# Linear attention with a gated unit: first-pass transfers queued behind weight loads, output-weight sums in steps, q feature steps spaced wider

## The chip, the cores and the metric

The kernel runs on one core of a Trainium2 chip. The metric is the device time of one execution in microseconds. TensorE (PE) multiplies into PSUM banks; VectorE (DVE), ScalarE (ACT) and GpSimd (POOL) do the element work; SyncE (SP) issues every transfer from one queue. Each engine works its queue off in the order in which the program was built.

## The reference

Both branches read the same layer-normed rows `xn` (2048 rows of 1024). The result is `x + s * silu(B)`.

```python
def _A_ref(x, wqkv, w_phi, wo):                  # x is xn
    q, k, v = ...(x @ wqkv)                      # 32 heads of 32
    pq = einsum("bhsd,hdf->bhsf", q, w_phi); pk = einsum(..., k, w_phi)
    phi_q = concatenate([softmax(pq), softmax(-pq)], -1)
    phi_k = concatenate([softmax(pk), softmax(-pk)], -1)
    kv = einsum("bhsf,bhsd->bhfd", phi_k, v); z = phi_k summed over s
    o = (phi_q @ kv) / (phi_q @ z + 1e-6)
    return o.reshape(B, S, D) @ wo
def _B_ref(x, w_gate, w_up, w_down):             # 1024 -> 3584 -> 1024
    return (sigmoid(x @ w_gate) * (x @ w_up)) @ w_down
```

## The kernel before, in words

**Products.** All large products are made by a two-by-two block scheme with seven products in place of eight. The products are called B11, B21, T2, T3, T4, T1 and B22, in this order; their operands are blocks or sums of blocks. fp32 operands are split in a high and a low part (`split`, L133 on ACT for the high part, L134 on DVE for the low one), and each product is three matmuls (`mm3`, L142 to L144), high by high, high by low, low by high. A group of twelve matmuls, four k steps of three, makes the share of one product in one PSUM bank; four groups, into banks 0 to 3 (named bank0_101 to bank3_104), make one operation. B11, T2, T3 and T1 start their banks anew; the others add to them. So before a bank is written again, its content must have been fetched by ACT or DVE.

**Stages.** The list `ops` sets TensorE's order: projection 0 (V, K and Q with seven operations each, for the first half of the rows), the first pass over the 14 tiles of the gated unit (two operations each, B11 and B21), projection 1 (the second half of the rows), the second and the third pass; then the down product and the attention output. The change touches the second half of projection 0 and the first pass.

**Ticks and steps.** After each group `tick` advances a clock and takes the entries of `plan` due then; `later(n, f)` makes such an entry n ticks ahead. What an entry issues is tied, by `tc.issue_after(last_mm[0])`, to TensorE's queue alone. `tc.issue_after(i)` orders only those instructions of its block that stand in the queue of i's engine. Otherwise a scheduler, with a model of the times, sets the order on each engine, so an entry's transfers and its element work can be put far ahead of their tick. `queue2` ties a step's transfers behind `last_load`, the last load or store so marked.

**Background steps around the change.**

- Q folds (`fold`, L350 on): the q weights times w_phi, summed on POOL (L291 to L294) and stored to `wf_d` (L345), in the first operations after the opening.
- Output weights (`o_sums`, L319 on): for k = 0 to 3, four blocks of `wo` are loaded into the halves of slots 52 and 53 (L322), split and stored as they are for three products, then summed on POOL and split and stored for the other four (L328). All of it is issued in one entry.
- Next rows (`x_stats` and `x_moments`): row loads (L178) and statistics (L694, L695) for the eight row tiles of the second half; then `x_pair`, four times, 12 ticks apart: loads (`x_in`, L724 and L727), scaling on DVE (`x_apply`, L733, four a pair), sums on POOL (L270, L234), stores.
- q features (`q_steps`, L808 on): 16 chains, 6.5 ticks apart: load, extremes (L546, L547), spread (L556, L557), exponentials on ACT (L560), sums and reciprocals (L565, L566), stores to `e_d` and `r_d`.

**Fetches.** In projection 0, `proj_out` fetches the banks: B11 and B21 on ACT (L520, L523), the others on DVE (`evac`, L517). In the first pass B11's banks are copied by ACT and stored (`keep_bank`, L1235, L1236), B21's banks 0 and 1 go through a sigmoid on ACT and banks 2 and 3 through a multiplication on DVE (`h_direct`, L1268, L1270). `glu_load` (L393) loads the pass's weights, up to four operations ahead.

Of the kernel before, what the change touches and what calls it, by code (L numbers as in the profile page):

```python
# [3 lines left out]

# [45 lines left out]
def hedgehog_glu_kernel(  # L50
# [66 lines left out]
    def whole(i):  # L117
        return slots[i].rearrange("p a n -> p (a n)")
# [36 lines left out]
    def tick():  # L155

        clock[0] += 1
        with tc.issue_after(last_mm[0]):
            glu_group()
        for f, a in sorted(plan.pop(clock[0], []), key=lambda fa: fa[0] is fetch_operand):  # L160
            with tc.issue_after(last_mm[0]):
                f(*a)

    side = deque()

# [121 lines left out]
    def w_sums(keep, a11, a12, a21, a22):  # L287

        for i, b in ((B11, a11), (B21, a12), (T4, a22)):
            keep(i, b)  # L290
        nc.gpsimd.tensor_add(a22, a21, a22)  # L291
        nc.gpsimd.tensor_sub(a21, a11, a21)
        nc.gpsimd.tensor_sub(a11, a22, a11)
        nc.gpsimd.tensor_sub(a12, a12, a11)  # L294
        for i, b in ((T2, a11), (T3, a21), (T1, a22), (B22, a12)):
            keep(i, b)
# [19 lines left out]

    o_split = Ring((54, 36, 37, 38))

    def o_sums(k, bs):  # L319

        for b, (f, h) in zip(bs, ((0, 0), (0, 1), (1, 0), (1, 1))):
            nc.sync.dma_start(b, wo[(k + 4 * h) * P:(k + 4 * h + 1) * P, f * HB:(f + 1) * HB])  # L322

        def keep(i, b):
            r = o_split.next()
            o = slots[r].bitcast(F32R)
            split((o[:, 0], o[:, 1]), b)
            nc.sync.dma_start(wo_d[i, k], whole(r))  # L328

        w_sums(keep, *bs)  # L330

    FB = ((0, 0), (0, 1), (1, 0), (1, 1))

# [49 lines left out]
    def glu_load(n):  # L383

        if n == len(ops) or ops[n][0] != "glu" or n in wraw:
            return True
        _, p, f, i = ops[n]
        if p == 1 and f in FLY:
            return True
        src = wg_d[summed.index(i), f] if i in summed else w_gu[f + NJ * (i == T4), int(i != B11)]  # L390
        if p == 0:
            r = gr.next()
            nc.sync.dma_start(whole(r), src)  # L393
            wraw[n] = halves(r)
            return True
        if (p, f, i) == (1, 0, T2):
            raw_free.extend(halves(41, 42, 39, 40))
        if len(raw_free) < 2:
            return False
        wraw[n] = [raw_free.popleft() for _ in range(2)]  # L400
        for s, o in enumerate(wraw[n]):
            last_load[:] = [nc.sync.dma_start(o, src[:, s * HB:(s + 1) * HB]).ins]
        if (p, f, i) == (1, 1, T4):
            spare.extend(halves(43, 44))
            raw_free.extend(spare)
        return True
# [152 lines left out]
    def exponentials(e):  # L559
        nc.scalar.activation(e, e, AF.Exp)  # L560
# [247 lines left out]
    def q_steps(at, t, hb):  # L808

        def load():  # L810
            p, e = hold[:] = qf_raw.next(), whole(qf_e.next())
            nc.sync.dma_start(p, qkv_d[Q, t, hb])

        def first():
            hold.append(extremes(f"q{t}{hb}", hold[0]))

        def rest():
            r = inverses(hold[2], hold[1])
            nc.sync.dma_start(r_d[t, hb], r)
            nc.sync.dma_start(e_d[t, hb], hold[1])  # L820

        hold = []
        for n, f in ((0, load), (4, first), (5, lambda: spread(hold[2], *hold[:2])), (7, lambda: exponentials(hold[1])),
                     (9, rest)):
            later(at + n, f)

    def q_task(t, hb):
# [459 lines left out]
    def begin_projection(c):  # L1287

        if c == 0:
            for k in range(4):  # L1290
                queue2(4 * (4 + 2 * k), o_sums, k, halves(52, 53))
            return
        for t in range(EARLY):
            k_steps(1 + 72 * t // EARLY, 0, t)
        for n in range(5):
            queue2(17 + 8 * n, glu_sums, *sums.popleft(), halves(43, 44))
# [30 lines left out]
    for n, (kind, c, what, i) in enumerate(ops):  # L1327
        if n < 8:
            continue
        ws = ready[n]  # L1330
        if kind == "proj":
            if n == 8 or (c and (what, i) == (PROJ[0], B11)):
                begin_projection(c)
            first_slot = (XO1 if c else XO)[i]
            xo = run(first_slot, 4)
            for u in range(4):
                if i in opening:
                    pbank[u] = pmm.next()
                us = slice(u * P, (u + 1) * P)
                for k in range(4):  # L1340
                    mm3(pbank[u], (xo[:, k, 0, us], xo[:, k, 1, us]), pair(ws[k]),
                        i in opening and k == 0, k == 3, skip_group_check=True)
                step()
                proj_out(c, what, i, u, pbank[u])
                if c and (what, i) == (Q, B22):
                    seed(0, u)
                if u < 3:
                    tick()
            flow["used"] += 4
            while prep():  # L1350
                pass
            if what == Q:
                if c == 0:
                    if i == T2:
                        load_outer(B11, 1)
                if c:
                    m = order.index(i)
                    if m < 6:
                        load_outer((T2, T2, T3, T3, T4, T4)[m], m % 2)
                    if i == T1:  # L1360
                        phase = 1
                        fetch(0)
                    if i == B22:
                        block("x1", 4, 4, F32)
                        m1 = halves(4, 5, 6, 7)
            tick()
            continue

        phase, f = c, what
        m = f * len(PASSES[phase]) + PASSES[phase].index(i)  # L1370
        if m == 0:
            if phase == 0:
                step(1000)
                for b in (0, 2, 6):
                    block(f"x{b}", 4 * b, 4, F32)
            begin_pass(phase)
        if (phase, i) in ((1, T2), (2, T1)):
            fetch(f + 1)
        for b in range(4):
            s, th = divmod(b, 2)  # L1380
            w = [h.rearrange("p (k m) -> p k m", m=P) for h in pair(ws[s])]
            xo = run(XG[i][th], 4)
            for k in range(4):
                mm3(banks[b], (w[0][:, k], w[1][:, k]), (xo[:, k, 0], xo[:, k, 1]),
                    i in (B11, T1) and k == 0, k == 3, skip_group_check=True)
            if i in (B11, T2, T3):
                keep_bank((B11, T2, T3).index(i), f, b)
            elif i == B21:
                h_direct(0, f, b)
            elif i == T4:  # L1390
                h_direct(0, f + NJ, b)
                seed(f + 1, b)
            elif i == T1:
                h_added(1, f + NJ, fetched[f][2], b)
            else:
                h_added(1, f, fetched[f][1], b)
            if th:
                flow["used"] += 1
                while prep():
                    pass  # L1400
            if b < 3:
                tick()
        if flow["item"] == len(items) and flow["made"] - flow["used"] < NW:
            hfree.extend(ws)
            while wfree and down_prep():
                pass

        if phase == 0:
            for o in {20: (B11,), 21: (B21,), 22: (T2,), 26: (T3, T4), 27: (T1, B22)}.get(m, ()):
                load_operand(XO1[o], xo_d[o])  # L1410
            if m == 27:
                block("p", 36, 2, F32R)
                block("p2", 38, 1, F32R)
        elif phase == 1 and (f, i) == (NJ - 2, T4):
            load_outer(T1, 0, lead=2)
        elif phase == 1 and f == NJ - 1:
            if i == T2:
                load_outer(T1, 1, lead=2)
                load_outer(B22, 0, lead=2)
            elif i == T3:  # L1420
                load_outer(B22, 1, lead=2)
            else:
                for b in (3, 5):
                    block(f"x{b}", 4 * b, 4, F32)
                uvfree.extend(halves(12, 13, 14, 15, 20, 21, 22, 23, 47, 51, 45, 46))
                hs_r.items = halves(48, 49, 50)
                phase = 2
                fetched.clear()
                fetch(0)
        elif phase == 2 and f == NJ - 2 and i == T1:  # L1430
            wfree.extend(range(16, 20))
        tick()
# [266 lines left out]
```

## Time and profile before

| | us |
|---|---|
| median of 3 runs | 2381.9 (2381.58 to 2384.36) |
| the profiled execution | 2384.26 |
| its span | 2382.5 |
| PE busy | 2364.6 (99%) |
| DVE busy | 1630.9 (68%) |
| ACT busy | 1046.5 (44%) |
| POOL busy | 957.6 (40%) |

A row of the timeline has the start, the duration, the engine, the line, the operation with its tiles, and in square brackets how long the engine was idle before it and who ended that. "<-issue" stands where the profile shows no waited-for event. SPq rows are transfers as SP issues them. A row of the waits has the engine and line, what it waited for, and us in total, times, and the longest. A row of the windows has the stretch, its length, then busy us (and instructions) of PE, PE's weight loads, DVE, ACT and POOL, the granted TensorE clock as a share of full speed, the DMA share and GB/s. A row of the groups has busy us and the mean ns of one. A row of the transfers has the count, KB each, and the median us from issue to landing.

### The profile page before, as it was taken

The page shows a single profiled execution, that of the slowest core. Times are in us where ns is not written, and L with a number is a line of the kernel's source. Part 1 is how long each engine was busy: PE and PEld are TensorE (multiplying, and loading weights), DVE is VectorE, ACT ScalarE, POOL GpSimd, SP SyncE. Part 2 cuts the span into 40 slices and gives each one's busy share as a digit, 9 for nine tenths or more (in the row PEclk, how much of TensorE's full clock was granted, in tenths as well). Part 3 has the DMA queues.
Part 4 walks back from the last instruction along what each step waited for, and adds up shares of the span by engine and source line. Part 5 has one row for each costly group of instructions (what it writes and reads, how often), then busy time and mean ns, then how long its engine had stood idle before and what let it go on. Part 6 is the DMA issues. An engine that isn't in the chain of part 4 may idle for free. (4 is left out here: it accounts for less than half of the span.)

```text
span 2382.5 us, 32056 instructions
## 1 busy us (share of the span) xinstructions
PE 2364.6 (99%) x10972; PEld 1970.0 (83%) x10972; DVE 1630.9 (68%) x2103; ACT 1046.5 (44%) x1595; POOL 957.6 (40%) x617
## 2 busy tenths in 40 slices
PE   9999999999999999999999999999999999999999
PEld 8887887888888888888888888888888888888887
DVE  8635847875577946577766633344888998877776
ACT  7333334364433545455555422223444334355553
POOL 0223227721032034444411587863333334423566
PEclk9999999999999999999999999999999999999999
DMA  8799989985587787677765999977666766876665
GB/s 294 251 319 339 372 332 346 340 302 188 176 287 259 256 292 243 212 255 249 234 203 189 345 382 379 346 266 252 213 220 227 234 221 209 283 264 235 200 208 180
DMA packets 287732, 631.45 MB, mean 265 GB/s; under 512 B 36688, under 2 KB 36944, under 8 KB 282960
## 3 DMA queue, kind: packets, MB, share of 16 engines
q1 hardware_dynamic: 287568, 629.40, 76.5%
q8 instruction: 86, 1.41, 0.2%
q14 instruction: 78, 0.64, 0.1%
HBM read 376.31 MB, written 252.97 MB: 264 GB/s over the span
## 5 line engine op out<-in xcount | busy, mean ns | idle before, releaser
L142 PE MATMUL bank<-x,w 128*128 128x512 f32 x2352 | 917.2, 390 | 4.6 <-ACT fc L1235 3.3
L143 PE MATMUL bank<-x,w 128*128 128x512 f32 x2352 | 916.6, 390 | 0.0
L144 PE MATMUL bank<-x,w 128*128 128x512 f32 x2352 | 914.9, 390 | 0.0
L134 DVE TENSOR_TENSOR w<-fa,w 128x512 fp32r<-128x512 f32 (+1 forms) x437 | 415.6, 957 | 206.4 <-ACT w L133 190.4
L133 ACT CAST w<-fa 128x512 fp32r<-128x512 f32 (+1 forms) x437 | 297.6, 685 | 543.0 <-PE bank L143 353.2
L142 PEld LDWEIGHTS bank<-x,w 128*128 128x128 f32 x2352 | 442.3, 188 | 97.3 <-ACT fc L1235 4.2
L144 PEld LDWEIGHTS bank<-x,w 128*128 128x128 f32 x2352 | 442.3, 188 | 92.3 <-DVE w L134 0.4
L143 PEld LDWEIGHTS bank<-x,w 128*128 128x128 f32 x2352 | 442.4, 188 | 90.6
L142 PE MATMUL bank<-w,x 128*128 128x512 f32 x708 | 278.8, 394 | 2.8 <-DVE fc L517 2.1
L143 PE MATMUL bank<-w,x 128*128 128x512 f32 x708 | 276.8, 391 | 0.9 <-DVE w L1092 0.9
L144 PE MATMUL bank<-w,x 128*128 128x512 f32 x708 | 276.6, 391 | 0.0
L142 PEld LDWEIGHTS bank<-w,x 128*128 128x128 f32 x708 | 133.4, 188 | 30.4 <-ACT p L133 2.5
L144 PEld LDWEIGHTS bank<-w,x 128*128 128x128 f32 x708 | 133.3, 188 | 27.9 <-DVE x L1082 0.3
L143 PEld LDWEIGHTS bank<-w,x 128*128 128x128 f32 x708 | 133.5, 189 | 27.5 <-DVE w L1092 1.3
L838 POOL TENSOR_TENSOR fc<-fc 128x1024 f32<-128x1024 f32 x32 | 81.6, 2551 | 176.1 <-ACT fc L560 126.5
L1235 ACT COPY fc<-bank 128x512 f32<-128x512 f32 x168 | 97.0, 583 | 93.1 <-PE bank L144 59.1
L1276 DVE TENSOR_TENSOR x<-x,bank 128x512 f32<-128x512 f32 x80 | 54.7, 686 | 117.0 <-PE bank L144 108.7
L134 DVE TENSOR_TENSOR x<-fa,x 128x512 fp32r<-128x512 f32 x112 | 116.4, 1039 | 20.4 <-ACT x L133 20.2
L850 POOL TENSOR_TENSOR fc<-fc,sa 128x1024 f32<-128x1024 f32 x32 | 70.4, 2199 | 92.5 <-DVE sa L847 92.5
L133 ACT CAST x<-fa 128x512 fp32r<-128x512 f32 x112 | 69.2, 618 | 60.2 <-DMA fa<-wd_d 26.2
L134 DVE TENSOR_TENSOR p<-fc,p 128x512 fp32r<-128x512 f32 (+1 forms) x65 | 55.4, 861 | 47.8 <-ACT p L133 40.6
L517 DVE TENSOR_TENSOR fc<-fc,bank 128x512 f32<-128x512 f32 x72 | 48.8, 680 | 43.4 <-PE bank L144 30.7
(311 smaller groups left out, 3153.8 us busy)
## 6 DMA issues: line engine op xcount, KB each, us to landing
m_d<-fc SPq DMA_DIRECT2D x168, 256.0 KB, 4.0
fa<-h_d SPq DMA_DIRECT2D x84, 512.0 KB, 4.2
x<-m_d SPq DMA_DIRECT2D x132, 256.0 KB, 5.2
fa<-wf_d SPq DMA_DIRECT2D x32, 1024.0 KB, 6.3
h_d<-fc SPq DMA_DIRECT2D x100, 256.0 KB, 5.0
fc<-e_d SPq DMA_DIRECT2D x48, 512.0 KB, 4.7
fc<-qkv_d SPq DMA_DIRECT2D x80, 256.0 KB, 4.2
fa<-wg_d SPq DMA_DIRECT2D x68, 256.0 KB, 5.1
```

Of the source, the lines that this page charges most:

```text
L133: nc.scalar.copy(o[0], src)
L134: i = nc.vector.tensor_sub(o[1], src, o[0].bitcast(F32))
L142: nc.tensor.matmul(o, a[0], b[0], start=first, stop=False, **kw)
L143: nc.tensor.matmul(o, a[0], b[1], start=False, stop=False, **kw)
L144: last_mm[:] = [nc.tensor.matmul(o, a[1], b[0], start=False, stop=last, **kw).ins]
L517: last_dve[:] = [nc.vector.tensor_add(y, x, b).ins]
L838: nc.gpsimd.tensor_mul(ez, e, zb)
L850: nc.gpsimd.tensor_mul(e3, e3, r2[:, :, None].to_broadcast([P, 32, DH]))
L1235: nc.scalar.copy(o, banks[b])
L1276: last_dve[:] = [nc.vector.tensor_add(us[b], us[b], banks[b]).ins]
```

## The change

It has three parts. First, while the first pass runs, the transfers of every entry of the plan are tied behind the last weight load (`loads_after`; `last_load` is now set by the pass's `glu_load` too). Second, the output weights are made in steps: `o_steps` puts loads, the three plain blocks, the sums, the stores and the last four splits on ticks 0, 5, 6, 7, 10, 11 and 12 behind a start, and the starts are 4, 16, 28 and 40 ticks into the stage, where they were 16, 24, 32 and 40. Third, the q steps take 13 ticks where they took 9, and the sums and the stores are entries of their own.

```diff
         for f, a in sorted(plan.pop(clock[0], []), key=lambda fa: fa[0] is fetch_operand):
-            with tc.issue_after(last_mm[0]):
+            with tc.issue_after(last_mm[0]), loads_after():
                 f(*a)
+    loads_fixed = []
+    def loads_after():
+        return tc.issue_after(last_load[0]) if loads_fixed else nullcontext()
...
-    def o_sums(k, bs):
-        for b, (f, h) in zip(bs, ((0, 0), (0, 1), (1, 0), (1, 1))):
-            nc.sync.dma_start(b, wo[(k + 4 * h) * P:(k + 4 * h + 1) * P, f * HB:(f + 1) * HB])
+    def o_steps(at, k, bs):
+        kept = []
+        def load():
+            for b, (f, h) in zip(bs, ((0, 0), (0, 1), (1, 0), (1, 1))):
+                nc.sync.dma_start(b, wo[(k + 4 * h) * P:(k + 4 * h + 1) * P, f * HB:(f + 1) * HB])
         def keep(i, b):
             r = o_split.next()
             o = slots[r].bitcast(F32R)
             split((o[:, 0], o[:, 1]), b)
-            nc.sync.dma_start(wo_d[i, k], whole(r))
-        w_sums(keep, *bs)
+            kept.append((i, r))
+        def stores():
+            for i, r in kept:
+                nc.sync.dma_start(wo_d[i, k], whole(r))
+            kept.clear()
+        def blocks_():
+            for i, b in ((B11, 0), (B21, 1), (T4, 3)):
+                keep(i, bs[b])
+        def two(*ib):
+            for i, b in ib:
+                keep(i, bs[b])
+        for n, f, *a in ((0, load), (5, blocks_), (6, w_sums, lambda i, b: None, *bs), (7, stores),
+                         (10, two, (T2, 0), (T3, 2)), (11, two, (T1, 3), (B22, 1)), (12, stores)):
+            later(at + n, f, *a)
...
             r = gr.next()
-            nc.sync.dma_start(whole(r), src)
+            last_load[:] = [nc.sync.dma_start(whole(r), src).ins]
...
-        def rest():
-            r = inverses(hold[2], hold[1])
-            nc.sync.dma_start(r_d[t, hb], r)
+        def sums():
+            hold.append(inverses(hold[2], hold[1]))
+        def keep():
+            nc.sync.dma_start(r_d[t, hb], hold[3])
             nc.sync.dma_start(e_d[t, hb], hold[1])
-        for n, f in ((0, load), (4, first), (5, lambda: spread(hold[2], *hold[:2])), (7, lambda: exponentials(hold[1])),
-                     (9, rest)):
+        for n, f in ((0, load), (5, first), (6, lambda: spread(hold[2], *hold[:2])), (9, lambda: exponentials(hold[1])),
+                     (11, sums), (13, keep)):
             later(at + n, f)
...
             for k in range(4):
-                queue2(4 * (4 + 2 * k), o_sums, k, halves(52, 53))
+                o_steps(4 + 12 * k, k, halves(52, 53))
...
             if n == 8 or (c and (what, i) == (PROJ[0], B11)):
+                loads_fixed.clear()
                 begin_projection(c)
...
             begin_pass(phase)
+            loads_fixed[:] = [True] if phase == 0 else []
```

In the changed file the lines named above have other numbers: L517 is L541, L546 and L547 are L570 and L571, L556 and L557 are L580 and L581, L560 is L584, L565 and L566 are L589 and L590, L733 is L757, L1235 is L1261, L1268 and L1270 are L1294 and L1296. L133 and L134 stay.

**VectorE at the end of K's products.** The rows with `bank` fetch T1's banks (fb) and then B22's (fc); rows that read `fa` split weights; the other L134 rows split output weights. Before:

```order
L517 TENSOR_TENSOR fb_0_99<-fb_0_99,bank0_101 128x512
L134 TENSOR_TENSOR fc_0_100<-fc_0_100 128x512
L517 TENSOR_TENSOR fb_0_99<-fb_0_99,bank1_102 128x512
L134 TENSOR_TENSOR p_0_95<-fc_0_100,p_0_95 128x512 x2
L517 TENSOR_TENSOR fb_0_99<-fb_0_99,bank2_103 128x512
L134 TENSOR_TENSOR w_0_94<-fa_0_97,w_0_94 128x2x512
L517 TENSOR_TENSOR fb_0_99<-fb_0_99,bank3_104 128x512
L134 TENSOR_TENSOR w_0_94<-fa_0_97,w_0_94 128x2x512
L134 TENSOR_TENSOR fc_0_100<-fc_0_100 128x512
L134 TENSOR_TENSOR p2_0_96<-fc_0_100,p2_0_96 128x512
L517 TENSOR_TENSOR fc_0_100<-fc_0_100,bank0_101 128x512
```

Now:

```order
L134 TENSOR_TENSOR p_0_95<-fc_0_100,p_0_95 128x512
L541 TENSOR_TENSOR fb_0_99<-fb_0_99,bank0_101 128x512
L134 TENSOR_TENSOR fc_0_100<-fc_0_100 128x512
L134 TENSOR_TENSOR p_0_95<-fc_0_100,p_0_95 128x512
L541 TENSOR_TENSOR fb_0_99<-fb_0_99,bank1_102 128x512
L541 TENSOR_TENSOR fb_0_99<-fb_0_99,bank2_103 128x512
L134 TENSOR_TENSOR p2_0_96<-fc_0_100,p2_0_96 128x512
L134 TENSOR_TENSOR w_0_94<-fa_0_97,w_0_94 128x2x512
L541 TENSOR_TENSOR fb_0_99<-fb_0_99,bank3_104 128x512
L134 TENSOR_TENSOR p_0_95<-fc_0_100,p_0_95 128x512
L134 TENSOR_TENSOR w_0_94<-fa_0_97,w_0_94 128x2x512
L134 TENSOR_TENSOR fc_0_100<-fc_0_100 128x512
```

The plain blocks' splits, three rows, have moved up: one stands ahead of T1's bank 0, three ahead of its bank 1; and the first split of a sum stands ahead of T1's bank 3 instead of B22's bank 0. On TensorE the products keep their order there; in Q's projection the first group of T3 now stands behind the second group of T2, where it stood behind T2's fourth.

**ScalarE in the first pass, the B11 operation of the fourth tile.** Rows with `bank` are copies (or, at fb, sigmoids); p and p2 are the two buffers of the q chains. Before:

```order
L1235 COPY fc_0_100<-bank0_101 128x512
L133 CAST w_0_94<-fa_0_97 128x512
L1235 COPY fc_0_100<-bank1_102 128x512
L1235 COPY fc_0_100<-bank2_103 128x512
L560 ACT_TABLE_LOAD
L560 ACTIVATE p_0_95<-p_0_95 128x1024
L560 ACTIVATE p2_0_96<-p2_0_96 128x1024
L133 CAST w_0_94<-fa_0_97 128x512
L1235 COPY fc_0_100<-bank3_104 128x512
L1268 ACT_TABLE_LOAD
L1268 ACTIVATE fb_0_99<-bank0_101 128x512
```

Now:

```order
L1261 COPY fc_0_100<-bank0_101 128x512
L133 CAST w_0_94<-fa_0_97 128x512
L1261 COPY fc_0_100<-bank1_102 128x512
L1261 COPY fc_0_100<-bank2_103 128x512
L133 CAST w_0_94<-fa_0_97 128x512
L1261 COPY fc_0_100<-bank3_104 128x512
L1294 ACT_TABLE_LOAD
L1294 ACTIVATE fb_0_99<-bank0_101 128x512
L584 ACT_TABLE_LOAD
L584 ACTIVATE p2_0_96<-p2_0_96 128x1024
L133 CAST w_0_94<-fa_0_97 128x512
L1294 ACT_TABLE_LOAD
```

The two exponentials between the third and the fourth copy are gone; single ones stand elsewhere, here behind the first sigmoid. ACT's queue has eight more table loads in all.

**VectorE in the first pass, the first two row pairs.** Before:

```order
L733 TENSOR_TENSOR fc_0_100<-fc_0_100,x6_2_2155 128x1024
L1270 TENSOR_TENSOR fc_0_100<-fc_0_100,bank3_104 128x512
L546 TENSOR_REDUCE stq10_2529<-p_0_95 128x16
L547 TENSOR_REDUCE stq10_2529<-p_0_95 128x16
L733 TENSOR_TENSOR x0_1_2153<-x0_1_2153,x6_2_2155 128x1024
L134 TENSOR_TENSOR w_0_94<-fa_0_97,w_0_94 128x512
L546 TENSOR_REDUCE stq11_2654<-p_0_95 128x16
L547 TENSOR_REDUCE stq11_2654<-p_0_95 128x16
L556 TENSOR_TENSOR p_0_95<-p_0_95,stq10_2529 128x16x32
L557 TENSOR_TENSOR p_0_95<-stq10_2529,p_0_95 128x16x32
L134 TENSOR_TENSOR w_0_94<-fa_0_97,w_0_94 128x512
L556 TENSOR_TENSOR p2_0_96<-p_0_95,stq11_2654 128x16x32
```

Now:

```order
L757 TENSOR_TENSOR fc_0_100<-fc_0_100,x6_2_2155 128x1024 x2
L570 TENSOR_REDUCE stq20_2804<-p_0_95 128x16
L571 TENSOR_REDUCE stq20_2804<-p_0_95 128x16
L134 TENSOR_TENSOR w_0_94<-fa_0_97,w_0_94 128x512
L580 TENSOR_TENSOR p_0_95<-p_0_95,stq20_2804 128x16x32
L581 TENSOR_TENSOR p_0_95<-stq20_2804,p_0_95 128x16x32
L757 TENSOR_TENSOR fc_0_100<-fc_0_100,x6_2_2155 128x1024
L1296 TENSOR_TENSOR fc_0_100<-fc_0_100,bank2_103 128x512
L589 TENSOR_REDUCE stq20_2804<-p_0_95 128x32
L757 TENSOR_TENSOR fc_0_100<-fc_0_100,x6_2_2155 128x1024
L590 RECIPROCAL stq20_2804<-stq20_2804 128x32
L1296 TENSOR_TENSOR fc_0_100<-fc_0_100,bank3_104 128x512
```

Before, the two pairs (fc is the first, x0 the second) alternated in one stretch with eight L733, of which the last two are shown, and two chains (stq10, stq11) ran side by side behind them. Now a pair's four L757 stand with one chain (stq20) between them, and the next pair's follow later.

2 lines of the change are left out of this document (1 added, 1 removed).

## The prediction

> **What bounds the kernel now.** I read the engines' shares first, then what TensorE waited for, then its timeline around the longest waits.
>
> ```profile
> PE 2364.6 (99%) x10972; PEld 1970.0 (83%) x10972; DVE 1630.9 (68%) x2103; ACT 1046.5 (44%) x1595; POOL 957.6 (40%) x617
> ...
> PE bank L142 <- ACT fc L1235: 3.3, 1, 3.3
> PE bank L142 <- DVE fc L517: 2.1, 1, 2.1
> ...
> PE bank L142 <- DVE ln L695: 0.7, 1, 0.7
> ```
>
> TensorE is busy for 2364.6 of 2382.5 us, so at most some 18 us of visible idle time can be won anywhere, plus what a lowered clock costs. The change touches the stretch from about 190 to 560 us (second half of projection 0, then the first pass); behind it TensorE's products are queued as before. Three waits lie there; I call them A (2.1), B (3.3) and C (0.7). All are of one kind: a product needs a PSUM bank whose old content ScalarE or VectorE has not yet fetched, because a background step stands ahead in that engine's queue.
>
> Wait A, on TensorE:
>
> ```profile
> 204.77 0.39 PE L144 MATMUL bank<-w,x 128*128 128x512 f32 x1
> ...
> 207.49 0.39 PE L144 MATMUL bank<-w,x 128*128 128x512 f32 x1
> 210.01 0.47 PE L142 MATMUL bank<-w,x 128*128 128x512 f32 x1 [2.14 <-DVE fc L517]
> 210.32 0.39 PE L143 MATMUL bank<-w,x 128*128 128x512 f32 x1
> ...
> 212.19 0.63 PE L142 MATMUL bank<-w,x 128*128 128x512 f32 x1
> ...
> 214.43 0.39 PE L142 MATMUL bank<-w,x 128*128 128x512 f32 x1
> ...
> 212.00:214.00 2.00, 2.00 (x6) 1.52 (x6) 2.00 (x4) 0.00 (x0) 0.00 (x0) 0.50 1.04 416
> ```
>
> Undisturbed, products start 0.227 us apart (12 starts, 2.72 us, from 204.77 to 207.49). Then 2.52 us pass between two starts: 2.29 lost. Behind it the granted clock stands at 0.50, and the 12 starts up to 214.43 take 4.42 us where 12 x 0.227 = 2.72 would do: 1.70 more. A costs 4.0 us. A wait of 1.3 us left the clock at 1.00:
>
> ```profile
> 165.44 1.13 PE L342 MATMUL bank<-fb,fb 128*128 128x128 f32 x8 [1.29 <-DMA fb<-wqkT]
> ...
> 164.00:168.00 4.00, 2.71 (x17) 2.32 (x17) 0.00 (x0) 0.00 (x0) 0.81 (x1) 1.00 1.07 297
> ```
>
> [...]
>
> Wait B, with ScalarE and VectorE beside it:
>
> ```profile
> 374.91 0.39 PE L144 MATMUL bank<-x,w 128*128 128x512 f32 x1
> 378.59 0.79 PE L142 MATMUL bank<-x,w 128*128 128x512 f32 x1 [3.30 <-ACT fc L1235]
> 384.96 0.39 PE L142 MATMUL bank<-x,w 128*128 128x512 f32 x1
> ...
> 371.39 1.28 ACT L560 ACT_TABLE_LOAD   x1 [6.30 <-DVE p L557]
> 372.69 1.06 ACT L560 ACTIVATE p<-p 128x1024 f32<-128x1024 f32 x1
> 376.49 1.06 ACT L560 ACTIVATE p<-p 128x1024 f32<-128x1024 f32 x1 [2.74 <-issue]
> 377.46 0.60 ACT L133 CAST w<-fa 128x512 fp32r<-128x512 f32 x1
> 377.96 0.58 ACT L1235 COPY fc<-bank 128x512 f32<-128x512 f32 x1
> ...
> 374.65 1.76 DVE L557 TENSOR_TENSOR p<-stq,p 128x512 f32<-128x512 f32 x1
> ...
> 360.00:380.00 20.00, 16.70 (x71) 13.50 (x70) 19.96 (x19) 7.51 (x10) 20.00 (x13) 0.95 0.91 311
> ...
> L733 DVE TENSOR_TENSOR x<-x,x 128x1024 f32<-128x1024 f32 x4 | 7.6, 1891 | 0.0
> L733 DVE TENSOR_TENSOR fc<-fc,x 128x1024 f32<-128x1024 f32 x4 | 6.4, 1610 | 0.0
> ```
>
> The gap is 374.91 to 378.59: 3.68 - 0.23 = 3.45 lost. The 15 starts to 384.96 take 6.37 where 3.41 would do: 2.96. B costs 6.4 us. Its cause: two q-feature chains run at once, and ScalarE's second exponential (376.49) waits for VectorE's spread (374.65 + 1.76), with the copy of the fourth bank (377.96) behind it. VectorE is late because it was full for 20 us (19.96 of 20.00): two whole row pairs' worth of L733, 14.0 us, fell between 343 and 376, while POOL was full as well.
>
> Wait C, two products in a row that were put close together in projection 0, and VectorE:
>
> ```profile
> 271.10 0.39 PE L143 MATMUL bank<-w,x 128*128 128x512 f32 x1
> 271.32 0.39 PE L144 MATMUL bank<-w,x 128*128 128x512 f32 x1
> 272.37 0.47 PE L142 MATMUL bank<-w,x 128*128 128x512 f32 x1 [0.66 <-DVE ln L695]
> ...
> 270.36 1.28 DVE L694 BATCH_NORM_STATS2 bn<-x 128x6 f32<-128x512 f32 x2
> 271.55 0.67 DVE L517 TENSOR_TENSOR fb<-fb,bank 128x512 f32<-128x512 f32 x1
> ```
>
> C costs 1.05 - 0.23 = 0.8 us: row statistics (270.36) stand ahead of the fetch (271.55). Together A, B and C are worth 11.2 us.
>
> **The change part by part.** No product, sum or transfer is added or removed; what moves is when each is queued.
>
> *Output weights in steps (A).* What made A:
>
> ```profile
> 189.97 1.70 SPq L345 DMA_DIRECT2D wf_d<-fc  x2
> ...
> 193.44 1.82 SPq L322 DMA_DIRECT2D fc<-wo  x4
> ...
> wf_d<-fc SPq DMA_DIRECT2D x6, 256.0 KB, 3.0
> fc<-wo SPq DMA_DIRECT2D x8, 256.0 KB, 4.9
> ...
> 197.19 0.62 ACT L133 CAST fc<-fc 128x512 fp32r<-128x512 f32 x1 [9.97 <-DMA fc<-wo]
> ...
> 205.82 1.77 DVE L134 TENSOR_TENSOR fc<-fc 128x512 fp32r<-128x512 f32 x1
> 207.73 1.54 DVE L134 TENSOR_TENSOR p<-fc,p 128x512 fp32r<-128x512 f32 x1
> 209.19 0.67 DVE L517 TENSOR_TENSOR fc<-fc,bank 128x512 f32<-128x512 f32 x1
> ```
>
> The first two splits of sums (205.82, 207.73), slow beside POOL, stand ahead of the fetch of bank 0 (209.19). Now the four block loads are queued 12 ticks earlier, but SP cannot issue them much earlier: they reuse halves that the last Q folds still store. So the first moves from 193.44 to perhaps 190.4 (right behind the store at 189.97), the last to about 194.4. But the first block's split now stands ahead of T1's bank 0 fetch. By a landing of 3.7 (193.44 to 197.19) to 4.9 us, a cast of 0.6 and a split of about 0.7, that fetch ends at 196.0 to 197.4. B22's first product needs it at 207.72 - 48 x 0.227 = 196.8: up to 0.6 lost. The third block's split precedes T1's bank 1 fetch: its half is stored at 191.4 at the latest (189.97 and two issues), free 3.0 later at 194.4; fetch done at 200.1 to 201.4, needed at 199.55: 0.5 to 1.8 lost. POOL starts its sums sooner, so the later splits come before they hurt. Left of A: 0.5 to 2.4, at worst all 4.0; I take 1.5, since each piece is nearest to the 1.29 that left the clock alone. Term: -2.5.
>
> *Transfers behind the last weight load (B, C).* The added edges bind SP's queue alone. They keep the next half's row loads and the row pairs from running ahead, so their VectorE and POOL work falls back to its own ticks. The statistics leave the end of projection 0, so C goes: -0.8 (cover: 270.36's two operations, 1.28, no longer precede the fetch). A row pair is due every 12 ticks of 12 products, 32.6 us, so a window like B's holds four L733 instead of eight: some 7 us of VectorE less, twice what B waited. What is queued behind the waiting transfers: h stores, bank stores and the next weight load; that load runs four tiles ahead.
>
> *q steps wider (B).* Exponentials now have three ticks after the spread (8.2 us) instead of two (5.4), and the two chains no longer stand as a pair between bank copies. B's missing time was 3.45; this alone gives 2.7 on ScalarE, and with the lighter VectorE I take all of it: -6.4 (bounds: 0, if a chain still blocks, to -6.4).
>
> *What it adds.* Eight more table loads, since exponentials alternate with sigmoids more often: 8 x 1.28 (371.39) = 10 us of ScalarE over the stretch below, where it has room.
>
> ```profile
> 286.00:590.00 304.00, 300.60 (x1320) 247.87 (x1319) 202.59 (x236) 139.09 (x196) 126.37 (x77) 0.99 0.85 305
> ```
>
> ScalarE works 139 of 304 us: free. In Q's T2 the next operation's bank 0 is now put after bank 1, as at C: one group, 2.7 us of cover. Nearest row: C's 0.8; bounds 0 to A's 4.0. And some shorter wait will show up where steps now meet: nearest 1.29 (165.44), bounds 0 to B's 6.4. Term: +2.1.
>
> Sum: -6.4 - 2.5 - 0.8 + 2.1 = -7.6. The profiled execution took 2384.26 us for a span of 2382.5; so 2376.7 for it. The median of the runs shown, 2381.9, lies 2.4 lower: 2374.3.
>
> **The rivals.** *Clean*: all three waits go and nothing comes: 2381.9 - 11.2 = 2370.7. For it: in the pass a bank has three groups, 8.2 us, of cover. Against: A's own queue.
>
> *B moves*: VectorE's work in the pass is the same (202.59 of 304 us), and sixteen chains still make ScalarE wait in its queue; one of them meets a row pair and costs B's price again. Or the transfers were behind the loads anyway, and little shifts. Then -2.5 - 0.8 + 2.1 = -1.2: 2380.7. Against: pairs and chains stand singly now.
>
> *Slower*: a q load now waits in SP's queue behind the weight load and stores that wait for POOL; the chain's first reductions stand in VectorE's queue ahead of the multiplications that free banks 2 and 3 (L1270), and every chain has its own such place. Where it is late by 8.2 us + 3.45, it costs B's 6.4 with its clock. From n such chains: -11.2 + 6.4 n; with three, +8.0: 2389.9. It decides from the third on (n above 2.5 passes +4.8). For it: POOL was full through 360 to 380. Against: four or more ticks lie between load and use.
>
> **How the numbers follow.** Forecast (two of three waits mostly gone) 0.43; clean 0.15; B moves 0.25; slower 0.17. A measurement here can tell 0.2%, 4.8 us. Forecast and clean lie below 2377.1: faster 0.58. "B moves" is no change: 0.25. Slower 0.17. The forecast's own range, with A's rest from 0.5 to 4.0 and the new waits from 0 to 3, is 2371 to 2378. Cases of both signs matter, so the range reaches from 2370 (clean) into the slower case, with about one in six left above: 2370 to 2386.
>
> **What would show it.** Right: no TensorE wait at L142 <- ACT L1235 above 1 us between 286 and 560 and a clock of 1.00 in every stretch there; no wait at the second to last operation of projection 0; near 197 to 202 one or two waits under 2 us in place of the one at 210; VectorE never full for 20 us in the pass. Wrong: a clock of 0.50 anywhere between 190 and 560, or a wait for L517 above 2 us in Q's T3, or waits for L1296 (the multiplications' line then) that recur with the chains.

## The result, and the profile after

| | before | changed |
|---|---|---|
| median on the same chip, 14 runs each | 2382.99 us | 2375.47 us |
| lowest to highest | 2378.76 to 2386.41 | 2371.16 to 2379.12 |
| profiled execution, its span | 2384.26, 2382.5 | 2374.87, 2373.1 |

The ratio is 0.9970, with a 95% interval from 0.9962 to 0.9978: 7.5 us less. Single runs of one kernel lie up to 8 us apart in this series, so two or three microseconds are read from profiles, and even those change from one execution to the next, as will be seen.

The busy times of the changed kernel, from its page:

```profile
PE 2360.2 (99%) x10972; PEld 1967.2 (83%) x10972; DVE 1610.1 (68%) x2103; ACT 1060.4 (45%) x1603; POOL 954.5 (40%) x617
```

The instructions are the same but for eight table loads (ACT 1595 to 1603). The two profiles' spans differ by 9.4 us, more than the medians. Where the lead arises is seen by setting equal TensorE rows of both timelines beside each other. Before, the last fold in projection 0 and a transpose behind the pass:

```profile
173.27 1.05 PE L342 MATMUL bank<-fb,fc 128*128 128x128 f32 x8
...
1004.28 1.03 PE L654 MATMUL bank<-ident,fc 128*128 128x128 f32 x8
```

The same two in the changed kernel:

```profile
170.40 1.13 PE L366 MATMUL bank<-fb,fc 128*128 128x128 f32 x8
...
992.75 1.03 PE L678 MATMUL bank<-ident,fc 128*128 128x128 f32 x8
```

2.9 us (173.27 - 170.40) were there before the first moved instruction: the waits for fold loads (1.29 and 0.48 before) happened not to occur, and one for a weight split near 110 us was 0.20 instead of 0.94. Behind the pass the lead is 11.5 us; so the changed stretch gave 8.7. Some 2.1 us of it went again in later stages, whose queues are the same in both kernels.

What TensorE waited for in the changed stretch, from its timeline:

```profile
194.14 0.39 PE L144 MATMUL bank<-w,x 128*128 128x512 f32 x1
194.71 0.47 PE L142 MATMUL bank<-w,x 128*128 128x512 f32 x1 [0.17 <-DVE fb L541]
...
197.28 0.39 PE L144 MATMUL bank<-w,x 128*128 128x512 f32 x1
198.49 0.50 PE L142 MATMUL bank<-w,x 128*128 128x512 f32 x1 [0.82 <-DVE fb L541]
...
266.85 0.39 PE L144 MATMUL bank<-w,x 128*128 128x512 f32 x1
267.89 0.47 PE L142 MATMUL bank<-w,x 128*128 128x512 f32 x1 [0.66 <-DVE fb L541]
```

Start to start, less 0.23, these lost 0.34, 0.98 and 0.81 us. In the pass there is no wait at all, and the stretch that held B reads:

```profile
360.00:380.00 20.00, 20.00 (x90) 16.56 (x89) 16.39 (x16) 10.50 (x14) 16.82 (x12) 1.00 1.03 379
```

PE is busy for all 20 us (16.70 before), DVE for 16.39 (19.96), POOL for 16.82 (20.00), the clock is 1.00 (0.95). The third wait stands at C's place. The row statistics have left, but VectorE's queue now has two splits of weights there (262.73), 2.2 us each while POOL works (4.30 of the 5 us from 262 to 267), and the fetch behind them ends at 267.75:

```profile
262.73 4.42 DVE L134 TENSOR_TENSOR w<-fa,w 128x1024 fp32r<-128x1024 f32 x2 [0.26 <-ACT w L133]
267.07 0.68 DVE L541 TENSOR_TENSOR fb<-fb,bank 128x512 f32<-128x512 f32 x1
```

### The profile page after: what moved, and what is told of

It is laid out like the page before. It is cut to its first block, busy times and chain, and to the rows that moved or that the text cites. A ratio compares the mean times of both kernels' runs of the same rounds, so it can differ in the third digit from the quotient of the medians.

```text
span 2373.1 us, 32026 instructions
## 1 busy us (share of the span) xinstructions
PE 2360.2 (99%) x10972; PEld 1967.2 (83%) x10972; DVE 1610.1 (68%) x2103; ACT 1060.4 (45%) x1603; POOL 954.5 (40%) x617
## 4 chain that ended last, share of the span: by engine, by line
PE 90%; DMA 4%; DVE 3%; POOL 1%; issue 1%; ACT 1%; SPq 0%; DVEq 0%; ACTq 0%; POOLq 0%
PE bank L142 28%; PE bank L143 28%; PE bank L144 28%; PE bank L642 1%; PE bank L932 1%; PE bank L908 1%; DMA wf_d<-fc 1%; DVE w L134 1%; DMA qkv_d<-fc 1%; PE bank L1182 1%; PE bank L366 1%; DMA fa<-wf_d 1%; DVE x L134 0%; DMA g_d<-fc 0%; DMA fc<-wo 0%
## 5 line engine op out<-in xcount | busy, mean ns | idle before, releaser
L134 DVE TENSOR_TENSOR w<-fa,w 128x512 fp32r<-128x512 f32 (+1 forms) x437 | 406.5, 935 | 216.9 <-ACT w L133 201.0
L133 ACT CAST w<-fa 128x512 fp32r<-128x512 f32 (+1 forms) x437 | 298.2, 685 | 552.4 <-PE bank L143 380.2
L1261 ACT COPY fc<-bank 128x512 f32<-128x512 f32 x168 | 97.5, 584 | 102.9 <-PE bank L144 67.4
L134 DVE TENSOR_TENSOR x<-fa,x 128x512 fp32r<-128x512 f32 x112 | 112.8, 1007 | 13.7 <-ACT x L133 13.6
L133 ACT CAST x<-fa 128x512 fp32r<-128x512 f32 x112 | 69.2, 618 | 47.8 <-DMA fa<-wd_d 27.3
L134 DVE TENSOR_TENSOR p<-fc,p 128x512 fp32r<-128x512 f32 (+1 forms) x65 | 54.1, 843 | 53.1 <-ACT p L133 52.6
L541 DVE TENSOR_TENSOR fc<-fc,bank 128x512 f32<-128x512 f32 x72 | 48.7, 681 | 42.9 <-PE bank L144 29.7
```

The costliest lines, as they stand in the source:

```text
L133: nc.scalar.copy(o[0], src)
L134: i = nc.vector.tensor_sub(o[1], src, o[0].bitcast(F32))
L541: last_dve[:] = [nc.vector.tensor_add(y, x, b).ins]
L1261: nc.scalar.copy(o, banks[b])
```

## The experiments

For each kernel the time that TensorE lost was added up from its timeline: distances between starts of 128x512 products beyond 0.227 us, in projection 0 (186 to 287 us) and in the pass (296 to 560 us). Waits and clock are added here. 1.78 us are taken off in the pass; every kernel has them at the row transposes near 339 to 354 us. By the first two rows the change gained 8.7 us in this stretch (5.0 + 6.8 - 3.1), which is the lead found above. One profiled execution each; the ratios are against the kernel before on the same chip.

| kernel | parts made | ratio, 95% interval | lost in projection 0 | lost in the pass |
|---|---|---|---|---|
| before | none | 1 | 5.0 | 6.8 |
| changed | 1, 2, 3 | 0.9970 (0.9962 to 0.9978) | 3.1 | 0 |
| changed, once more | 1, 2, 3 | 0.9973 (0.9962 to 0.9983) | 5.8 | 0 |
| transfers alone | 1 | 0.9968 (0.9956 to 0.9980) | 3.8 | 0 |
| output weights alone | 2 | 1.0005 (0.9996 to 1.0014) | 5.2 | 6.6 |
| q steps alone | 3 | 0.9995 (0.9986 to 1.0004) | 4.5 | 5.5 |
| without transfers | 2, 3 | 1.0007 (0.9997 to 1.0017) | 4.4 | 6.7 |
| without output weights | 1, 3 | 0.9969 (0.9956 to 0.9981) | 4.4 | 0 |
| without q steps | 1, 2 | 0.9966 (0.9954 to 0.9978) | 5.3 | 0 |
| rows' transfers alone | half of 1 | 0.9966 (0.9954 to 0.9978) | 2.3 | 1.2 |
| other transfers alone | half of 1 | 1.0002 (0.9994 to 1.0011) | 8.3 | 6.3 |
| steps two ticks later | 1, 2, 3 | 0.9971 (0.9960 to 0.9981) | 5.5 | 0 |
| splits behind fetches | 1, 2, 3 | 0.9962 (0.9950 to 0.9974) | 2.4 | 0 |

### The three parts, each alone

Transfers alone: the changed kernel with `o_sums` and the old q steps put back.

```diff
-                o_steps(4 + 12 * k, k, halves(52, 53))
+                queue2(4 * (4 + 2 * k), o_sums, k, halves(52, 53))
...
-        for n, f in ((0, load), (5, first), (6, lambda: spread(hold[2], *hold[:2])), (9, lambda: exponentials(hold[1])),
-                     (11, sums), (13, keep)):
+        for n, f in ((0, load), (4, first), (5, lambda: spread(hold[2], *hold[:2])), (7, lambda: exponentials(hold[1])),
+                     (9, rest)):
```

> The kernel before with the first part alone: transfers of the first pass's steps queued behind the last weight load; output weights and q chains as before. My theory (VectorE full for 20 us made wait B, since two row pairs ran ahead together): the row pairs fall back to their ticks, VectorE is not full for 20 us between 340 and 380 us, and wait B (3.45 us idle, 2.96 us of lowered clock) shrinks to under 1 us with the clock at 1.00: 2383.0 - 6.4 = about 2376.6. A (4.0 us) stays. The statistics leave the end of projection 0, so C (0.8 us) loses its cause. Rival (the narrow spacing of the q steps made B): a wait of over 2 us for ScalarE's copy of the fourth bank with the clock at 0.50 stays in the first pass, and the time stays at 2382 to 2383.

Measured: 2376.40 against 2384.82 us. B is gone, with no wait in the pass; A stayed (2.36 us, this time with the clock at 1.00), and 1.29 us were lost at C's place, where the statistics no longer stood. This part alone gives the whole gain that the times can show.

Output weights alone: the old q steps, and the switch for the transfers left out.

```diff
-            loads_fixed[:] = [True] if phase == 0 else []
```

> The kernel before with the second part alone: the output weights' sums in steps, begun 12 ticks earlier; transfers and q chains as before. My theory: wait A (2.29 us idle, 1.70 us of clock) goes, and two short waits near 194 and 198 us stand in its place (0.34 and 0.98 us in the changed kernel) with the clock at 1.00: -2.7 us, about 2380.3; B's 6.4 us stay. Rival (A needs the other parts too, or was a chance of that one execution): a wait over 2 us for the same fetch stays and the time stays at 2383; or B goes as well because the order in the pass has shifted, about 2374.

Measured: 2384.44 us, no gain. A's wait went, but 1.19 (at 189) and 1.83 us (at 200) came, and 1.09 us were lost at C's place (272); and B's one wait became four of 1.18, 1.13, 1.46 and 2.29 us, the first and the last of them here:

```profile
319.73 0.50 PE L142 MATMUL bank<-x,w 128*128 128x512 f32 x1 [1.02 <-ACT fc L1259]
...
463.08 0.50 PE L142 MATMUL bank<-x,w 128*128 128x512 f32 x1 [2.13 <-ACT fc L1259]
```

q steps alone: `o_sums` put back, and the same switch left out.

> The kernel before with the third part alone: q steps spaced wider; transfers and output weights as before. My theory: the row pairs still run ahead and VectorE is still full for about 20 us between 340 and 380 us, but the exponential has 2.7 us more, so that of B's 3.45 us idle some 0.7 us is left and the clock stays at 1.00: -5.6 us, about 2377.4. A stays at 4.0 us, C at 0.8 us. Rival (only the transfers cure B): a wait of over 2 us with a clock of 0.50 stays in the first pass, 2382 to 2383.

Measured: 2383.13 us; the rival holds. B stands unaltered. ScalarE's queue in this kernel:

```profile
368.68 1.06 ACT L566 ACTIVATE p<-p 128x1024 f32<-128x1024 f32 x1
372.48 1.06 ACT L566 ACTIVATE p<-p 128x1024 f32<-128x1024 f32 x1 [2.74 <-issue]
373.44 0.60 ACT L133 CAST w<-fa 128x512 fp32r<-128x512 f32 x1
373.95 0.57 ACT L1243 COPY fc<-bank 128x512 f32<-128x512 f32 x1
```

and TensorE behind it:

```profile
374.58 0.50 PE L142 MATMUL bank<-x,w 128*128 128x512 f32 x1 [3.29 <-ACT fc L1243]
```

These are the rows that the prediction showed of before, 4.0 us earlier: the same 2.74 us between the two exponentials, the same 3.45 us lost; only the slow stretch behind it was shorter (1.7 us lost against 2.96). The ticks had moved; the queues had hardly moved.

### The three parts, each left out

Each is the changed kernel with one of the edits above.

> The changed kernel without its first part: the transfers of the first pass's steps are queued freely again; output weights in steps and wide q steps stay. If the transfers have a share in B that the spacing cannot give: row pairs run ahead again, VectorE is full for some 20 us between 340 and 390 us, and a wait of 0.5 us or more comes back in the first pass: 2376 to 2379. If the spacing alone is enough: no TensorE wait above 0.3 us in the pass, 2375.5. C's place: with the statistics back at the end of projection 0, its wait stays at about 0.8 us, whoever stands ahead.

Measured: 2385.67 against 2382.88 us. Both cases fell short: the four waits of "output weights alone" are all there (1.24, 1.14, 1.48, 2.23 us), and no gain shows. At C's place 1.07 us were lost.

> The changed kernel without its second part: the output weights' sums at once, from tick 16 on, as before. My theory: wait A comes back with its 2.29 us idle and 1.70 us of lowered clock, and the short waits near 194 and 198 us go: +2.7 us, about 2378.2; the first pass stays free of waits. Rival (A was a chance of one execution): no wait above 1 us near 205 to 210 us, 2375 or less.

Measured: 2376.28 us. A is back (2.55 us, with 1.68 of clock), as the first case said, yet the time isn't the slower one: in its place nothing is lost at 194, 198 and 268 us.

> The changed kernel without its third part: narrow q steps, with the transfers behind the last weight load and output weights in steps. If VectorE's relief alone cures B: no TensorE wait above 1 us in the first pass, clock 1.00, 2375.5 to 2376.5. If the spacing is what counts: a wait of 2 us or more for ScalarE's copy of the fourth bank comes back, with a clock of 0.50 behind it, about 2382.

Measured: 2375.00 us, no wait in the pass. Narrow q steps do no harm once the transfers are held.

### Which transfers

`loads_after` was given the entry's function; on top of "transfers alone" it holds either those of the input rows or all others.

```diff
+    def loads_after(f):
+        bound = loads_fixed and f.__name__ in ('x_stats', 'x_pair', 'x_keep', 'outer_keep', 'x_sums_keep')
+        return tc.issue_after(last_load[0]) if bound else nullcontext()
```

> The kernel before with half of the first part: only the transfers of the input rows' steps (statistics' loads, the row pairs' loads and stores) are queued behind the last weight load; those of the q steps and the gate weights' sums stay free. If the row pairs running ahead are what fills VectorE: B's wait (3.45 us) is gone, VectorE is not full between 340 and 380 us, 2376 as with the whole part. If the q loads are: B stays at 3 us or more, 2383.

Measured: 2374.90 against 2383.19 us, and one wait of 1.12 us in the pass (at 450).

> The kernel before with the other half of the first part: only the transfers of the q steps and of the other steps are queued behind the last weight load; those of the input rows stay free. If the row pairs are the cause of B: VectorE still full for some 20 us between 340 and 380 us, waits of 2 us or more in the first pass, 2382 to 2384. If the q loads are: no wait above 1 us there, 2376.

Measured: 2383.86 us, with B as before:

```profile
378.47 0.79 PE L142 MATMUL bank<-x,w 128*128 128x512 f32 x1 [3.30 <-ACT fc L1242]
```

So it is the rows' transfers that have to be held for B to go. The row pairs' loads in SP's queue, before:

```profile
286.56 0.33 SPq L724 DMA_DIRECT2D x<-xT  x1
290.95 1.45 SPq L724 DMA_DIRECT2D x<-xT  x1
312.38 0.33 SPq L724 DMA_DIRECT2D fc<-xT  x1
314.28 0.33 SPq L724 DMA_DIRECT2D fc<-xT  x1
411.08 0.55 SPq L724 DMA_DIRECT2D fc<-xT  x1
415.10 0.85 SPq L724 DMA_DIRECT2D x<-xT  x1
416.00 0.71 SPq L724 DMA_DIRECT2D fc<-xT  x1
418.32 0.33 SPq L724 DMA_DIRECT2D x<-xT  x1
```

and in the changed kernel:

```profile
319.90 0.33 SPq L748 DMA_DIRECT2D fc<-xT  x1
321.70 0.33 SPq L748 DMA_DIRECT2D fc<-xT  x1
360.57 0.94 SPq L748 DMA_DIRECT2D x<-xT  x1
366.00 0.47 SPq L748 DMA_DIRECT2D x<-xT  x1
397.46 0.33 SPq L748 DMA_DIRECT2D fc<-xT  x1
399.88 0.33 SPq L748 DMA_DIRECT2D fc<-xT  x1
426.38 0.67 SPq L748 DMA_DIRECT2D x<-xT  x1
430.67 0.38 SPq L748 DMA_DIRECT2D x<-xT  x1
```

Unbound, the loads of two pairs are out by 314 us, and those of the other two by 418; bound, one pair follows the other after 29 to 41 us, the 12 ticks asked for being 32.6. VectorE's scalings follow: before, eight L733 stand between 349 and 366 us and eight between 429 and 451; now the L757 stand in fours, from 340, 368, 407 and 440 us on. The kernels with this spacing are those without a wait above 1.2 us in the pass: changed, transfers alone, without output weights, without q steps, rows' transfers alone, and the three of the next section. The unheld queue also kept the q chains back. The first loads of their inputs before:

```profile
324.84 1.78 SPq L812 DMA_DIRECT2D p<-qkv_d  x2
...
344.20 0.32 SPq L812 DMA_DIRECT2D p<-qkv_d  x1
345.40 0.32 SPq L812 DMA_DIRECT2D p<-qkv_d  x1
```

and now:

```profile
282.48 0.46 SPq L836 DMA_DIRECT2D p<-qkv_d  x1
...
294.29 0.33 SPq L836 DMA_DIRECT2D p<-qkv_d  x1
```

Before, they come two by two, the first 42 us later (324.84 - 282.48), so two chains ran side by side in B. Late or paired q loads aren't enough for a wait, though. With the rows' transfers alone held, they still come two by two:

```profile
287.86 0.96 SPq L819 DMA_DIRECT2D p<-qkv_d  x2
...
303.44 0.36 SPq L819 DMA_DIRECT2D p<-qkv_d  x1
305.42 0.32 SPq L819 DMA_DIRECT2D p<-qkv_d  x1
```

B is gone there. In "splits behind fetches" the first two leave together at 311.69 us, with no wait in the pass; in "output weights alone" the first leaves as early as 295.90, and four waits came. In these profiles the waits of 2 us and more in the pass go with the bunched row pairs.

### Can the rest of A be had?

Steps two ticks later: `o_steps(6 + 12 * k, ...)`.

> The changed kernel with the output weights' steps begun two ticks (5.4 us) later: 6 + 12k instead of 4 + 12k. My theory: the first splits of output weights no longer stand ahead of the two bank fetches near 194 and 198 us, so their 0.34 and 0.98 us go; POOL's last sums begin 5.4 us later, so the two weight splits that they slow to 2.2 us each no longer stand ahead of the fetch at 267.1 us, and its 0.81 us go too: about -2 us against the changed kernel, 2373.4. Rival (any place of these steps meets some fetch): waits of the same sum, 2 us, at other products, 2375.5; at worst one above 2 us with a clock of 0.50, 2379.

Measured: 2377.61 against 2384.82 us; the rival's case. 1.99, 0.68 and 2.29 us were lost at 200, 209 and 271 us. The loads of the first step left at 189.06 us and not 5.4 us later than the changed kernel's 188.48: they reuse halves of the folds and stand between the folds' last stores in SP's queue, so the start tick is not what sets them.

The changed kernel once more:

> The changed kernel once more, unaltered, for a second profiled execution and as the others' neighbour on the same chip. If what is left of A hangs on when transfers land, the waits near 194, 198 and 268 us differ from those of its first profile (0.34, 0.98, 0.81 us) by a microsecond or more, as the same code did in the kernel with the gaps (2.30 at 198.9 and 1.54 at 268.6 us); if they are fixed by the order, they come out within 0.3 us of it. No wait above 0.3 us between 286 and 560 us either way; 2375.5.

Measured: 2377.83 against 2383.19 us. Projection 0 came out at 0.51 (194 us), 2.31 (199), 0.96 (208), 0.96 (240) and 0.37 us (270). The same queues, another execution:

```profile
198.99 0.50 PE L142 MATMUL bank<-w,x 128*128 128x512 f32 x1 [2.15 <-DVE fb L541]
```

In projection 0 the queues of all engines are the same in four of the profiles: the changed kernel's two, that without q steps and that with gaps below. They lost 0.98, 2.31, 2.30 and 2.30 us at this product, so the first profile's 0.98 was a lucky draw, and only behind the third of them did the clock fall (to 0.50). A part of the difference is the split right ahead of this fetch: it took 0.68 us in the first profile and 1.73, beside POOL, in the second.

Splits behind fetches:

```diff
+            with tc.issue_after(fetched_bank[0]):
+                split((o[:, 0], o[:, 1]), b)
...
+            last_dve[:] = fetched_bank[:] = [nc.vector.tensor_add(y, x, b).ins]
...
+                o_steps(16 + 9 * k, k, halves(52, 53))
```

The second half of a step is on ticks 8 and 9 here.

> The changed kernel with one thing more: each split of output weights is placed in VectorE's queue behind the latest bank fetch of the projection, and the four steps begin at ticks 16 + 9k. My theory: the waits near 194 to 209 us and at 268 us (2.1 us in the changed kernel's profile, 3.8 in the kernel with the gaps, 5.0 with the steps two ticks later) come from splits that stand ahead of a fetch; with the fetches first they fall to under 0.8 us together, and the time is 2 to 3 us under the changed kernel's on the same chip, about 2373. Rival (the weight splits slowed beside POOL do it, not the output weights' own): a wait of 0.8 us or more stays near 268 to 272 us, and the time is that of the changed kernel within 1 us.

Measured: 2374.77 against 2383.19 us, runs from 2373.28 to 2375.72. The waits at 194 to 209 and at 268 us are gone; one of 1.64 us appeared at 235, where a ScalarE copy stands behind casts of output and other weights:

```profile
235.08 0.50 PE L142 MATMUL bank<-w,x 128*128 128x512 f32 x1 [1.49 <-ACT fc L548]
```

It was 3.1 us under the changed kernel's median in the same series, but the intervals overlap (0.9950 to 0.9974 and 0.9962 to 0.9983), so a gain over the changed kernel isn't shown.

### What idle time lowers the clock

```diff
+                with tc.issue_after(stalled[0]) if stalled else nullcontext():
...
+            if phase == 0 and 14 <= m < 28 and b == 1:
+                with tc.issue_after(last_mm[0]):
+                    nc.tensor.matmul(banks[6][:, :P], ident, ident, start=True, stop=True)
+                for _ in range((1, 2, 3, 4, 5, 6, 7)[m % 7]):
+                    nc.scalar.copy(banks[7], banks[6])
+                stalled[:] = [nc.tensor.matmul(banks[7][:, :P], ident, ident, start=True, stop=True).ins]
```

> The changed kernel with work added: in each of the last 14 operations of the first pass (from about 430 us on) TensorE writes a spare bank behind its second group, ScalarE copies that bank to another 1 to 7 times (each about 0.6 us), and TensorE's next product waits for the last copy. Nothing is left out. It measures which idle time lowers the clock. My theory, from A, B and C: gaps up to about 1.6 us leave the granted clock at 1.00; from about 2.3 us on the next products run at 0.50 for some 3 to 5 us, costing 1.7 to 3 us more. [...]

The gaps in TensorE's timeline, those of the same length beside each other:

```profile
446.29 0.49 PE L1421 MATMUL bank<-ident 128*128 128x128 f32 x2 [1.27 <-ACT bank L1420]
459.76 0.49 PE L1421 MATMUL bank<-ident 128*128 128x128 f32 x2 [1.84 <-ACT bank L1420]
475.41 0.49 PE L1421 MATMUL bank<-ident 128*128 128x128 f32 x2 [2.43 <-ACT bank L1420]
...
581.62 0.49 PE L1421 MATMUL bank<-ident 128*128 128x128 f32 x2 [1.83 <-ACT bank L1420]
595.67 0.49 PE L1421 MATMUL bank<-ident 128*128 128x128 f32 x2 [2.44 <-ACT bank L1420]
611.68 0.49 PE L1421 MATMUL bank<-ident 128*128 128x128 f32 x2 [2.75 <-ACT bank L1420]
```

and the granted clock (third number from the end) behind the second to sixth of them, and behind the gaps of four copies in the first round (491.10) and of five and six in the second (627.80 and 644.80):

```profile
460.60:463.60 3.00, 3.00 (x8) 2.31 (x7) 0.00 (x0) 0.00 (x0) 0.72 (x1) 0.50 1.01 389
476.00:479.00 3.00, 3.00 (x15) 2.47 (x14) 0.65 (x2) 0.31 (x1) 0.00 (x0) 1.00 0.83 315
491.10:494.40 3.30, 3.30 (x9) 2.60 (x8) 1.16 (x1) 0.84 (x1) 0.00 (x0) 0.51 0.34 72
582.20:585.20 3.00, 3.00 (x15) 2.48 (x14) 0.00 (x0) 0.32 (x1) 0.00 (x0) 1.00 0.11 42
597.00:600.20 3.20, 3.20 (x9) 2.52 (x8) 0.00 (x0) 0.00 (x0) 0.00 (x0) 0.50 0.02 5
612.20:615.20 3.00, 3.00 (x14) 2.44 (x14) 0.27 (x1) 0.23 (x1) 0.00 (x0) 1.00 0.87 334
627.80:631.10 3.30, 3.30 (x9) 2.61 (x8) 0.00 (x0) 0.00 (x0) 0.00 (x0) 0.50 0.00 0
644.80:648.00 3.20, 3.20 (x9) 2.50 (x8) 0.00 (x0) 0.00 (x0) 0.00 (x0) 0.50 0.00 0
```

1.84 us lowered the clock, 1.83 didn't; 2.44 did, 2.43 and even 2.75 didn't; behind the other three gaps it stood at 0.51, 0.50 and 0.50. The theory doesn't hold: from 1.8 to 2.8 us the length alone doesn't decide. (This kernel took 2444.72 us, with the work added.)

## Why the prediction came out right

**The time was right, and so was the place of most of it; the credit among the parts was not.** 2374.3 was forecast and 2375.47 measured, -7.6 and -7.5 us by the medians.

**B, -6.4: right in size, half right in cause.** The pass lost 6.8 us before, 6.4 of them by B, and at most one wait of 1.1 us in every kernel that holds the rows' transfers. The paragraph on transfers named the mechanism (row pairs fall back to their own ticks, half as many L733 at a time) and then let the q steps share B: "this alone gives 2.7 on ScalarE". That step failed. Alone, the wider steps gave 0.9995 of the time, and B stood row for row. The 5.4 and 8.2 us were counted from the table of ticks, but both chains ran late, on loads that came late and in pairs from SP's queue, and ScalarE's queue kept its order there whatever the ticks said. The two parts didn't add; one alone did all of it.

**"VectorE full" was a sign and not the cause.** The forecast's mark "VectorE never full for 20 us in the pass" was met by the changed kernel (16.39 of 20), but the one with splits behind fetches shows this, with no wait at all in the pass:

```profile
340.00:380.00 40.00, 40.00 (x184) 33.10 (x183) 39.50 (x43) 20.87 (x30) 24.60 (x16) 1.00 0.92 338
```

39.50 of 40 us, and TensorE doesn't notice. What hurt in B was narrower: a ScalarE operation that waited for VectorE's late result stood ahead of a bank copy. Why a full VectorE makes that result late in one kernel and not in another stays open.

**A, -2.5: not borne out.** The order at the place was read rightly; two short waits near 194 and 198 came, at the products named and within the bounds given (0.34 in 0 to 0.6, 0.98 in 0.5 to 1.8) in the first profile. But the second profile has 2.31 there, outside. The six profiles of the table with the old sums lost 2.3 to 8.3 us in projection 0 (mean 4.7); the seven with the steps, at whatever ticks, 2.4 to 5.8 (mean 4.5). Neither these nor the ratios show a gain: the part moved the splits from ahead of one fetch to ahead of others. The nearest row, 1.29 that left the clock alone, was no bound for a wait that came out between 0.98 and 2.31 us with the same queues.

**C, -0.8: wrong in the first profile, and chance in others.** The statistics left, and two weight splits beside POOL took their place for 0.81 us, so the sign "no wait at the second to last operation of projection 0" failed. The second profile lost 0.37 there, transfers alone 1.29, and the kernel without output weights nothing. With the statistics still there, q steps alone lost nothing and other transfers alone 2.23. So the statistics weren't what decided. "Cover" was claimed by naming what leaves a queue, without reading what moves up.

**New waits, +2.1.** In the pass there were none; in projection 0 they are A's and C's successors. T3's bank 0 in Q, put behind one group, cost nothing: in the first profile only one start between 199 and 266 us came late, by 0.28 us (at 217.95), and that was B21's. The eight table loads were free, as said: ScalarE was busy for 138.28 of the 274 us from 286 to 560, and TensorE never waited for it there.

**The rivals.** "B moves" was refuted by every kernel that holds the rows' transfers, but it is what the other two parts do without the first: four waits for B's one, at the same price. "Slower" didn't come: no wait for L1296 stands in the pass of the changed kernel, and q loads came earlier, not later. "Clean" was nearest in the pass.

So of the sum, the pass gave -6.8 for the -6.4 (B, and 0.4 us of a short wait near 466); projection 0 gave some -0.2 by the two means, for A's and C's -3.3; and the allowance of +2.1 for new waits is already in these two. That -7.0 lies within the measured interval (-9.1 to -5.2 us), but that the forecast met the median was partly luck: the allowance offset gains that aren't there.

## What to carry to other kernels

When background steps are placed by ticks, check that the ticks are in force: a step whose load may be issued freely can run ahead or late by the order of the transfer queue, as here the loads of two row pairs (both out by 314 us) and of the first q chains (42 us late), and its element work can bunch with the next step's (eight L733 between 349 and 366 us). Tie the loads of such steps to the stream's own loads in that queue; here one such tie on one group of transfers was worth all that three edits brought. And undo each part alone before giving it credit, with a second profile of the same kernel: a wait of 1 us in one execution was 2.3 in the next.

## What the runs showed of the hardware

In the kernel with gaps the granted clock stood at 0.50 or 0.51 in five of the eight stretches listed above, and at 1.00 in three. The five hold 8 or 9 products in 3.00 to 3.30 us, the three 14 or 15 in 3.00. In the first of the five the products start 0.43 us apart instead of 0.227:

```profile
460.63 0.63 PE L144 MATMUL bank<-x,w 128*128 128x512 f32 x1
461.06 0.63 PE L142 MATMUL bank<-x,w 128*128 128x512 f32 x1
461.49 0.63 PE L143 MATMUL bank<-x,w 128*128 128x512 f32 x1
```

At half the clock over 3.00 to 3.30 us each stretch cost some 1.5 to 1.65 us, an estimate from these rows. What decides between 1.83 and 2.75 us, where the length doesn't, isn't shown. The waits that came by themselves agree: in the profiles of all these kernels six of thirteen waits of 2.2 to 2.6 us in projection 0 and the pass lowered the clock. 2.29 (before), 2.55 (without output weights), 2.23 and 2.58 us (other transfers alone) did, 2.31 (changed, once more) and 2.36 us (transfers alone) didn't. So A is worth 2.3 or 4.0 us by chance, and by that share 2.3 + 6/13 x 1.7 = 3.1 on average, an estimate with A's 1.70 for the slow stretch; the prediction's 4.0 took one draw for the price.
